# Linear-attention block and ReLU MLP on one core: four layer-norm tiles on GpSimd and a new order of all engines

## The chip, the cores and the metric

The kernel runs on one core of a Trainium2 chip. A core has a tensor engine (PE) with its weight loads (PEld), a vector engine (DVE), a scalar engine (ACT), GpSimd (POOL) and a sync engine (SP), which here issues all DMAs. The metric is the device time of one launch in microseconds (us). Before the change the median of three runs is 174.51 us (174.1 to 175.42).

## The reference

The input x has 2048 rows of 512 bf16 numbers. The block is a linear attention with 32 heads of 16 columns on the layer norm of x, and then a ReLU MLP with 1792 hidden columns on the layer norm of the sum h; both layer norms have no weights.

```python
def _layernorm(x, axis=-1, eps=1e-5):
    ...
    return (x - m) / jnp.sqrt(v + eps)
...
phi = lambda t: jnp.where(t > 0, t + 1, jnp.exp(t)) + 1e-6
pq, pk = phi(q), phi(k)
kv = jnp.einsum("bhsd,bhse->bhde", pk, v)
z = jnp.einsum("bhsd->bhd", pk)
num = jnp.einsum("bhqd,bhde->bhqe", pq, kv)
den = jnp.einsum("bhqd,bhd->bhq", pq, z)[..., None] + 1e-6
...
h = x + _A_ref(_layernorm(x, axis=-1), A_wqkv, A_wo)
h2 = h + _B_ref(_layernorm(h, axis=-1), B_w1, B_w2)   # relu(LN(h) @ w1) @ w2
```

## The kernel before

The 2048 rows are 16 tiles of 128 rows, and four chunks of four tiles. Nothing loops: the text ORDER lists some 560 words, and the last lines of the kernel call one function per word (`S.4` calls `op_S(4)`, L215). Each engine runs its own words in the order in which they stand; between engines only data, buffers and PSUM banks make one wait for the other. The last number of a PE word is its PSUM bank, of which there are eight.

First layer norm, tile t: `lx` loads x; `S` and `A` (DVE) take mean and variance; `R` (ACT, a logarithm and an exponential, here called the deviation) gives 1/deviation for one or two tiles; `N` (DVE, L229) writes (x minus mean) times 1/deviation into ln_nat, which is the tile h_nat in the profile. The normalised tile is then transposed into lnT: tiles 0 to 5 by PE (`T`) with a copy out of PSUM by ACT (`E`) or DVE (`V`), tiles 6 to 15 by a DMA that SP issues (`X`, L269).

Keys: `K` (PE, four 128x512 matmuls) gives x wk of a tile; `F` (ACT exponential), `U` (ACT ReLU), `M` (DVE minimum) and `D` (DVE sum) make phi of it; `G` (PE, four matmuls) gathers the product of the normalised tile and phi(k) in banks 4 to 7 over all tiles. Queries: `Q`, `qF`, `qU`, `qM`, `qD` do the same by chunk and quarter of the columns. `z` sums phi(k) over rows, `kv`, `kx`, `m` and `mD` fold wv, the head mask and wo into the matrix m_sb. `masks` (POOL) builds the three masks that `kx`, `zr`, `zh` and `rp` read.

The denominators: for chunk 0 by `d4`, `dl4`, `dx4` and `rp`; for the others `d` (PE), `dl` (ACT logarithm), `dx` (ACT exponential), `dm` (DVE product). `h` (PE) multiplies with m_sb, `hD` (DVE) adds x. Second layer norm: `s`, `a`, `r`, and `n` takes the mean off; `t` with `e` or `v`, or the DMA `x`, transpose. The MLP: `p` (PE, four matmuls for one of 14 blocks of 128 hidden columns of a chunk), evacuated in pairs by ACT (`pA`) or DVE (`pD`) with ReLU; `f` (PE) multiplies with w2; `fo` (DVE) scales by 1/deviation and adds h; `fd` stores a tile. Weight loads are `lk`, `lq`, `lv`, `lo`, `l1`, `l2`; `warm` are matmuls on zeros at the start.

SP issues the DMAs in one row in the order of the words. Each of its DMAs also takes one of eight completion counters in turn.

Of the kernel before, what the change touches and what calls it, by code (L numbers as in the profile page):

```python
# [18 lines left out]
table const masks warm.9.7 lx.0.1 S.0 lx.1.1 S.1 A.0 A.1 lx.2.2 S.3 S.2 R.1.1 R.0.1 lx.4.2 lk.0.2 lk.2.2  # L19
lx.6.2 A.3 A.2 N.0.2.2 N.0.0.2 N.1 R.2.2 N.2 N.3 warm.1.7 T.0.3.2.2 T.0.0.0.2 T.1.1 T.2.2 E.0.2.2 E.1 V.0.0.2  # L20
T.3.3 E.2 E.3 K.0.0 S.4 S.5 A.4 A.5 K.1.1 K.3.3 K.2.2 F.0.1 R.4.2 U.0.1 F.1.1 S.6 S.7 M.0.1 A.7 A.6 N.4 R.6.2
U.1.1 lx.8.4 T.4.0 D.0.1 G.0 M.1.1 N.5 N.7 T.5.1 E.4 U.2.1 F.2.1 E.5 F.3.1 U.3.1 K.4.0 D.1.1 S.9 N.6 S.8 G.1
M.2.1 A.9 A.8 D.2.1 R.8.2 K.5.1 F.4.2 U.4.2 M.3.1 S.10 N.8 D.3.1 N.9 M.4.2 S.11 D.4.2 lq.2.2 lq.0.2 lx.12.4
A.11 A.10 X.7 X.6 X.9 X.8 lv.0.2 G.2 K.7.3 K.6.2 G.3 F.6.2 R.10.2 U.6.2 S.12 S.13 M.6.2 N.11 N.10 A.13 A.12
D.6.2 R.12.2 G.4 G.5 K.9.1 K.8.0 F.8.2 U.8.2 S.14 N.13 A.14 N.12 S.15 M.8.2 A.15 D.8.2 X.11 X.10 R.14.2 N.14
N.15 lv.2.2 X.12 X.13 X.14 X.15 l1.0.2 l2.0.7 l2.7.7 lo.2.2 lo.0.2 l1.2.2 G.6 G.7 K.11.3 K.10.2 F.10.2 U.10.2
G.8 G.9 K.12.0 K.13.1 F.12.2 U.12.2 M.10.2 D.10.2 G.10 K.14.2 K.15.3 F.14.2 M.12.2 M.14.2 D.12.2 Q.0.1.1
Q.0.0.0 G.11 G.12 qF.0.0.2 qU.0.0.2 U.14.2 G.13 Q.0.3.1 Q.0.2.0 qM.0.0.2 D.14.2 qD.0.0.2 G.14 G.15 z.1.2
qF.0.2.2 qU.0.2.2 gD.0.2 z.0.2 z.2.2 z.3.2 zc qM.0.2.2 gA.2.2 zr zh qD.0.2.2 Q.1.1.3 Q.1.0.2 qF.1.0.2 qU.1.0.2
kv.1.4 kv.0.4 kv.2.4 kv.3.4 kx qM.1.0.2 Q.1.3.1 m.1.5 m.0.4 d4.0.3 m.3.7 m.2.6 Q.1.2.0 Q.2.0.2 dl4.0 mD.0.2  # L30
# [490 lines left out]
```

## Time and profile before

| | us |
|---|---|
| median of three runs (range) | 174.51 (174.1 to 175.42) |
| profiled execution, span from first to last instruction | 173.1 |
| PE busy | 165.8 |
| weight loads busy | 77.7 |
| DVE busy | 99.7 |
| ACT busy | 72.3 |
| POOL busy | 4.7 |

Of the profiled execution only its span is recorded; the runs' median lies 1.4 us above it. Busy time is the sum of the instructions' spans. A matmul's span (379 ns for 128x512) overlaps the next one's, so the spacing of matmuls, not their mean, tells how long a group takes: four 128x512 matmuls follow each other within 0.863 us once PE is at speed (2.16 us for ten in the chain of work that ended last), and the warm-up matmuls within 0.43 us each. The granted TensorE clock is 1.00 in every stage. An instruction on DVE or ACT likewise starts up to 0.1 us before the one ahead of it has ended. In the views, L12 is line 12 of the kernel, an arrow names what ended an engine's idle time, and SPq is SP's queue of DMA issues.

### The profile page before, as it was taken

What the parts mean: (1) busy time and instruction counts of PE and PEld (TensorE: products, weight loads), DVE (VectorE), ACT (ScalarE), POOL (GpSimd) and SP (SyncE); (2) the same over time, 40 slices, a digit from 0 to 9 for tenths busy, and PEclk for the clock granted to TensorE, in tenths of its full rate; (3) what the DMA queues carried; (4) which work ended last, traced back from release to release, by engine and by line L of the source; (5) the groups of instructions that cost most, each with busy time, mean ns of one, the idle gap of its engine ahead of it and who ended that gap; (6) DMA issues with size and microseconds to landing.
All of it is one profiled execution on the core that took longest, in us unless ns stands there. A gap on an engine that the chain in (4) does not pass through costs nothing.

```text
span 173.1 us, 2263 instructions
## 1 busy us (share of the span) xinstructions
PE 165.8 (96%) x856; PEld 77.7 (45%) x872; DVE 99.7 (58%) x208; ACT 72.3 (42%) x112; POOL 4.7 (3%) x21
## 2 busy tenths in 40 slices
PE   7699989999999999999999999999999999999992
PEld 2244434446444544444444444444444444444551
DVE  3899965154799949796338089455769402500032
ACT  2499755666586794213057210006623000363100
POOL 7300000000000000000000000000000000000000
PEclk9999999999999999999999999999999999999999
DMA  5883456899000000002220000462001320010021
GB/s 139 280 307 61 77 132 152 255 364 360 4 0 0 4 0 0 0 0 61 61 64 30 0 2 0 108 78 91 0 0 30 65 60 0 30 62 0 0 80 45
DMA packets 19979, 13.00 MB, mean 75 GB/s; under 512 B 12544, under 2 KB 18816, under 8 KB 19968
## 3 DMA queue, kind: packets, MB, share of 16 engines
q1 hardware_dynamic: 19968, 12.85, 26.5%
q8 instruction: 7, 0.11, 0.3%
q14 instruction: 4, 0.03, 0.1%
HBM read 7.86 MB, written 2.10 MB: 58 GB/s over the span
## 4 chain that ended last, share of the span: by engine, by line
PE 85%; DVE 7%; DMA 5%; issue 1%; SPq 1%
PE bk L470 28%; PE bk L450 28%; PE bk L435 8%; PE bk L285 8%; PE bk L329 5%; PE bk L277 4%; DVE st L215 4%; DMA lnT<-h_nat 2%; DMA x_nat<-in_A_x_dram 2%; DVE h_nat L229 2%; PE bk L415 2%; PE bk L337 1%; DVE eb L302 1%; PE bk L374 1%; PE bk L248 1%
## 5 line engine op out<-in xcount | busy, mean ns | idle before, releaser
L450 PE MATMUL bk<-lnT,w_sb 128*128 128x512 bf16 x220 | 50.9, 379 | 0.2
L470 PE MATMUL bk<-w_sb,at 128*128 128x512 bf16 (+1 forms) x233 | 49.8, 366 | 0.3
L470 PEld LDWEIGHTS <-at 128*128 128x128 bf16 x238 | 23.3, 98 | 25.3
L450 PEld LDWEIGHTS <-w_sb 128*128 128x128 bf16 x224 | 21.9, 98 | 26.5
L456 ACT ACTIVATE at<-bk 128x1024 bf16<-128x1024 f32 x14 | 14.2, 1022 | 41.0 <-PE bk L450 22.3
L478 DVE SCALAR_TENSOR_TENSOR gT<-bk,rstd,h_nat 128x512 bf16<-128x512 f32 (+1 forms) x17 | 11.8, 716 | 30.4 <-PE bk L470 17.0
L461 DVE TENSOR_SCALAR at<-bk 128x1024 bf16<-128x1024 f32 x14 | 17.1, 1221 | 14.4 <-PE bk L450 14.4
L295 ACT ACTIVATE eb<-bk 128x1024 bf16<-128x1024 f32 (+1 forms) x18 | 16.6, 930 | 10.4 <-PE bk L277 6.1
L418 ACT ACTIVATE ld<-bk,eps 128x512 f32<-128x512 f32 x12 | 7.7, 693 | 27.7 <-PE bk L415 27.7
L298 ACT ACTIVATE rb<-bk 128x1024 bf16<-128x1024 f32 (+1 forms) x18 | 16.6, 927 | 1.3 <-DVE pqs L408 0.7
L277 PE MATMUL bk<-wk_sb,lnT 128*128 128x512 bf16 x64 | 15.3, 379 | 0.6 <-DMA lnT<-h_nat 0.6
L441 DVE TENSOR_TENSOR h_nat<-bk,x_nat 128x512 bf16<-128x512 f32 x16 | 10.7, 682 | 8.6 <-PE bk L435 8.6
L435 PE MATMUL bk<-m_sb,pqs 128*128 128x512 bf16 x62 | 15.2, 379 | 0.1
L285 PE MATMUL bk<-lnT,wq_sb 128*128 128x512 bf16 x61 | 14.7, 379 | 0.1
L329 PE MATMUL bk<-at,h_nat 128*128 128x512 bf16 x55 | 13.2, 379 | 0.1
L215 DVE BATCH_NORM_STATS2 st<-x_nat 128x6 f32<-128x512 bf16 x16 | 10.5, 680 | 2.7 <-DMA x_nat<-in_A_x_dram 2.7
L302 DVE TENSOR_SCALAR eb<-eb 128x1024 bf16<-128x1024 bf16 (+1 forms) x18 | 6.9, 389 | 7.0 <-ACT eb L295 7.0
L217 DVE BATCH_NORM_STATS2 st<-h_nat 128x6 f32<-128x512 bf16 x16 | 10.7, 683 | 0.2
L435 PEld LDWEIGHTS <-pqs 128*128 128x128 bf16 x64 | 6.3, 98 | 7.5
L277 PEld LDWEIGHTS <-lnT 128*128 128x128 bf16 x64 | 6.1, 98 | 7.9 <-DMA lnT<-h_nat 1.0
L329 PEld LDWEIGHTS <-h_nat 128*128 128x128 bf16 x64 | 6.2, 98 | 7.3
L285 PEld LDWEIGHTS <-wq_sb 128*128 128x128 bf16 x64 | 6.0, 98 | 6.9 <-issue 0.2
(63 smaller groups left out, 95.2 us busy)
## 6 DMA issues: line engine op xcount, KB each, us to landing
w_sb<-in_B_w_dram SPq DMA_DIRECT2D x4, 896.0 KB, 8.1
out_dram<-gT SPq DMA_DIRECT2D x15, 128.0 KB, 1.8
x_nat<-in_A_x_dram SPq DMA_DIRECT2D x2, 512.0 KB, 7.0
x_nat<-in_A_x_dram SPq DMA_DIRECT2D x3, 256.0 KB, 4.0
wk_sb<-in_A_wqkv_dram SPq DMA_DIRECT2D x2, 256.0 KB, 4.8
wq_sb<-in_A_wqkv_dram SPq DMA_DIRECT2D x2, 256.0 KB, 6.8
wv_sb<-in_A_wqkv_dram SPq DMA_DIRECT2D x2, 256.0 KB, 3.3
wo_sb<-in_A_wo_dram SPq DMA_DIRECT2D x2, 256.0 KB, 8.9
```

Of the source, the lines that this page charges most:

```text
L215: op_S = lambda t: nc.vector.bn_stats(out=st[:, t, :], in_=x_nat[:, t, :])
L277: nc.tensor.matmul(bk[:, b, :], lhsT=lnT[c][:, kd, j * P : (j + 1) * P], rhs=wk_sb[:, kd, :], start=(kd == 0), stop=(kd == KD - 1),)
L285: nc.tensor.matmul(bk[:, b, :], lhsT=wq_sb[:, kd, j * P : (j + 1) * P], rhs=lnT[c][:, kd, :], start=(kd == 0), stop=(kd == KD - 1),)
L295: nc.scalar.activation(out=buf(eb, kind, i, n), in_=bank(at_bank[kind, i], n), func=ACT.Exp)
L298: nc.scalar.activation(out=buf(rb, kind, i, n), in_=bank(at_bank[kind, i], n), func=ACT.Relu)
L329: nc.tensor.matmul(bk[:, KD + kd, :], lhsT=ln_nat[:, t, kd * P : (kd + 1) * P], rhs=pk(t)[:, 0, :], start=(t == 0), stop=(t == NT - 1),)
L435: nc.tensor.matmul(bk[:, b, :], lhsT=pqs[:, (c * KD + jb) % NQ, j * P : (j + 1) * P], rhs=m_sb[:, jb, :], start=(jb == 0), stop=(jb == KD ...
L450: nc.tensor.matmul(bk[:, b, :], lhsT=w1_sb[:, kd, f * P : (f + 1) * P], rhs=lnT[c][:, kd, :], start=(kd == 0), stop=(kd == KD - 1),)
L456: nc.scalar.activation(out=acts[c % 2][:, f : f + n, :], in_=bank(at_bank["p", c, f], n), func=ACT.Relu)
L461: nc.vector.tensor_scalar(out=acts[c % 2][:, f : f + n, :], in0=bank(at_bank["p", c, f], n), scalar1=0.0, scalar2=None, op0=ALU.max,)
L470: nc.tensor.matmul(bk[:, b, 0 : w * P], lhsT=acts[c % 2][:, f, j * P : (j + 1) * P], rhs=w2_sb[:, f, k * P : (k + w) * P], start=(f == 0), ...
L478: nc.vector.scalar_tensor_tensor(out=o_t[:, t % NO, cols], in0=bk[:, at_bank["f", t, k], 0 : w * P], scalar=rstd2[:, t : t + 1], in1=h_nat ...
```

## The change

Two functions are new in use: `ng` writes minus the mean of a tile on GpSimd, and `Np` normalises a tile on GpSimd as (x plus minus mean) times 1/deviation, in one instruction of 128x512 bf16 with two per-row scalars. Tiles 4, 6, 7 and 8 take this way; the other twelve stay on DVE. `ng` stands in the order for twelve tiles, of which eight (5, 9 to 15) have no `Np`, so that their result is read by nothing. `masks` moves from the start of GpSimd's row to behind the `ng` of tile 14.

All the other words are put in a new order, with other banks in places. In the row of PE the kinds and numbers of instructions stay. Tiles 2 and 5 are now copied out of PSUM by DVE (`V`) instead of ACT, and tile 0 in both halves by ACT. Of the 28 evacuations of the MLP's hidden blocks ACT does 19 and DVE 9, where each did 14. SP loads the last four tiles of x ahead of wq; wq's two halves, wv's two and one of wo's now stand between the DMA transposes, where before only wv's two did. `dx4` writes to the place of wk, which is no longer used then, instead of rd.

The diff also adds functions and options that the new order doesn't call (a sum for `z` on DVE, a broadcast of denominators through DRAM, `p` in column halves, `dm` over several blocks); they are left out here.

```diff
 ORDER = """
-table const masks warm.9.7 lx.0.1 S.0 lx.1.1 S.1 A.0 A.1 lx.2.2 S.3 S.2 R.1.1 R.0.1 lx.4.2 lk.0.2 lk.2.2
-lx.6.2 A.3 A.2 N.0.2.2 N.0.0.2 N.1 R.2.2 N.2 N.3 warm.1.7 T.0.3.2.2 T.0.0.0.2 T.1.1 T.2.2 E.0.2.2 E.1 V.0.0.2
-T.3.3 E.2 E.3 K.0.0 S.4 S.5 A.4 A.5 K.1.1 K.3.3 K.2.2 F.0.1 R.4.2 U.0.1 F.1.1 S.6 S.7 M.0.1 A.7 A.6 N.4 R.6.2
-U.1.1 lx.8.4 T.4.0 D.0.1 G.0 M.1.1 N.5 N.7 T.5.1 E.4 U.2.1 F.2.1 E.5 F.3.1 U.3.1 K.4.0 D.1.1 S.9 N.6 S.8 G.1
-M.2.1 A.9 A.8 D.2.1 R.8.2 K.5.1 F.4.2 U.4.2 M.3.1 S.10 N.8 D.3.1 N.9 M.4.2 S.11 D.4.2 lq.2.2 lq.0.2 lx.12.4
-A.11 A.10 X.7 X.6 X.9 X.8 lv.0.2 G.2 K.7.3 K.6.2 G.3 F.6.2 R.10.2 U.6.2 S.12 S.13 M.6.2 N.11 N.10 A.13 A.12
-D.6.2 R.12.2 G.4 G.5 K.9.1 K.8.0 F.8.2 U.8.2 S.14 N.13 A.14 N.12 S.15 M.8.2 A.15 D.8.2 X.11 X.10 R.14.2 N.14
-N.15 lv.2.2 X.12 X.13 X.14 X.15 l1.0.2 l2.0.7 l2.7.7 lo.2.2 lo.0.2 l1.2.2 G.6 G.7 K.11.3 K.10.2 F.10.2 U.10.2
-G.8 G.9 K.12.0 K.13.1 F.12.2 U.12.2 M.10.2 D.10.2 G.10 K.14.2 K.15.3 F.14.2 M.12.2 M.14.2 D.12.2 Q.0.1.1
-Q.0.0.0 G.11 G.12 qF.0.0.2 qU.0.0.2 U.14.2 G.13 Q.0.3.1 Q.0.2.0 qM.0.0.2 D.14.2 qD.0.0.2 G.14 G.15 z.1.2
-qF.0.2.2 qU.0.2.2 gD.0.2 z.0.2 z.2.2 z.3.2 zc qM.0.2.2 gA.2.2 zr zh qD.0.2.2 Q.1.1.3 Q.1.0.2 qF.1.0.2 qU.1.0.2
-kv.1.4 kv.0.4 kv.2.4 kv.3.4 kx qM.1.0.2 Q.1.3.1 m.1.5 m.0.4 d4.0.3 m.3.7 m.2.6 Q.1.2.0 Q.2.0.2 dl4.0 mD.0.2
-dx4.0 qU.1.2.2 qF.1.2.2 mD.2.2 rp.0.1.5 rp.0.2.6 rp.0.3.7 rp.0.0.4 Q.2.1.3 Q.2.3.1 Q.2.2.0 qU.2.0.2 qU.2.2.2
-qF.2.0.2 qF.2.2.2 qD.1.0.2 rm.0.0.2 qM.1.2.2 rm.0.2.2 qD.1.2.2 h.1.5 h.0.4 hD.1 s.1 hD.0 h.3.7 Q.3.0.2 h.2.6
-...
-p.3.1.1 p.3.0.0 pA.3.0.2 f.10.6.7.7 pD.3.2.2 p.3.4.0 p.3.5.1 p.3.6.2 p.3.7.3 fo.9 pA.3.4.2 p.3.9.1 fo.10 fo.11
-pA.3.6.2 fd.9 fd.11 fd.10 p.3.8.0 f.12.4.0.7 pA.3.8.2 p.3.12.0 p.3.10.2 p.3.13.1 pA.3.12.2 r.12.4 p.3.11.3
-pA.3.10.2 f.13.5.0.7 f.13.5.7.7 f.12.4.7.7 fo.12 fd.12 fo.13 fd.13 f.15.7.0.14.0.2 f.14.6.0.7 f.14.6.7.7
-fo.15.0.2 fo.14 fd.15.0.2 fd.14 f.15.4.0.14.2.2 fo.15.2.2 fd.15.2.2
+lx.1.1 const lx.0.1 S.1 table A.1 S.0 A.0 R.1.1 R.0.1 N.1 lx.2.2 warm.9.7 T.1.5 S.3 N.0.0.2 S.2 A.3 A.2 lk.0.2
+lx.4.2 T.0.0.0.2 warm.1.7 N.0.2.2 E.1 lk.2.2 T.0.3.2.2 S.4 R.2.2 E.0.0.2 E.0.2.2 K.1.2 N.3 lx.6.2 S.5 A.4 A.5
+lx.8.4 N.2 T.3.1 E.3 ng.4.1 R.4.2 S.7 K.0.7 Np.4 T.2.5 K.3.3 F.0.1 N.5 T.5.1 U.0.1 U.1.1 A.7 V.2 T.4.4 K.2.7
+S.6 V.5 A.6 E.4 R.6.2 F.2.1 F.1.1 U.2.1 S.8 M.0.1 S.9 lx.12.4 D.0.1 M.1.1 D.1.1 A.9 M.2.1 A.8 ng.7.1 ng.6.1
+Np.6 Np.7 K.4.0 K.5.1 X.6 U.3.1 F.3.1 G.0 D.2.1 X.7 R.8.2 G.1 G.2 S.10 M.3.1 A.10 S.11 A.11 D.3.1 N.9 U.4.2
+F.4.2 R.10.2 S.12 ng.8.1 K.6.2 K.7.3 N.11 M.4.2 D.4.2 S.15 N.10 S.13 G.3 U.6.2 Np.8 X.8 lq.2.2 K.8.0 G.4 A.15
+A.12 A.13 F.6.2 R.12.2 M.6.2 N.13 N.12 X.9 G.5 K.9.1 F.8.2 lq.0.2 X.11 D.6.2 S.14 A.14 R.14.2 U.8.2 X.10
+lv.2.2 X.12 K.11.3 G.6 N.15 K.10.2 N.14 M.8.2 D.8.2 G.7 X.13 lv.0.2 X.14 lo.2.2 X.15 l2.7.7 U.10.2 F.10.2
+K.12.0 K.13.1 G.8 K.14.2 G.9 K.15.3 U.12.2 F.12.2 l2.0.7 l1.0.2 lo.0.2 l1.2.2 M.10.2 D.10.2 F.14.2 M.12.2
+D.12.2 M.14.2 Q.0.1.1 G.10 ng.13.1 G.11 U.14.2 D.14.2 z.3.2 z.1.2 z.0.2 z.2.2 G.12 Q.0.0.0 qF.0.0.2 qU.0.0.2
+G.13 G.14 G.15 gA.2.2 zc gD.0.2 qM.0.0.2 qD.0.0.2 Q.0.2.0 Q.0.3.1 qF.0.2.2 kv.3.4 kv.2.4 ng.10.1 ng.5.1
+ng.14.1 masks kv.1.4 kv.0.4 ng.15.1 qU.0.2.2 Q.1.1.3 Q.1.0.2 kx qM.0.2.2 zh qD.0.2.2 zr ng.11.1 ng.9.1 ng.12.1
+m.3.7 m.2.6 d4.0.1 m.1.5 m.0.4 qF.1.0.2 Q.1.2.0 dl4.0 qU.1.0.2 mD.2.2 Q.1.3.1 Q.2.1.3 mD.0.2 dx4.0 rp.0.2.6
+rp.0.3.7 rp.0.0.4 qM.1.0.2 Q.2.0.2 rp.0.1.5 qU.1.2.2 qF.1.2.2 qD.1.0.2 rm.0.2.2 rm.0.0.2 qM.1.2.2 qF.2.0.2
+qU.2.0.2 Q.2.3.1 Q.2.2.0 h.2.7 h.0.2 qU.2.2.2 qF.2.2.2 h.3.5 h.1.4 d.1.1.6 qD.1.2.2 hD.2 s.2 hD.0 Q.3.1.3
+Q.3.0.2 dl.1.1 a.2 hD.3 s.0 hD.1 s.3 a.0 n.2 Q.3.3.1 dx.1.1 Q.3.2.0 t.2.5 qU.3.0.2 a.3 s.1 a.1 n.1 n.0 n.3
+t.1.7 qF.3.0.2 t.0.3 e.2 t.3.2 e.0 qF.3.2.2 qU.3.2.2 v.1 d.1.0.4 d.1.2.6 d.1.3.7 v.3 dl.1.3 dl.1.2 qM.2.0.2
+qD.2.0.2 p.0.1.3 p.0.0.2 dm.1.1 qM.2.2.2 pD.0.0.2 qM.3.0.2 d.2.1.5 dx.1.3 dl.2.1 dx.1.2 dl.1.0 dx.2.1 dx.1.0
+p.0.2.0 p.0.3.1 p.0.4.2 p.0.5.3 pD.0.2.2 dm.1.2 qD.2.2.2 qM.3.2.2 p.0.6.0 p.0.7.1 pA.0.4.2 dm.1.3 dm.1.0
+d.2.0.2 dl.2.0 h.4.3 d.2.2.5 d.2.3.6 h.7.7 pD.0.6.2 dx.2.0 h.6.2 dl.2.3 dl.2.2 hD.4 qD.3.2.2 qD.3.0.2 dm.2.1
+hD.6 p.0.9.3 d.3.0.6 h.5.1 d.3.1.5 p.0.8.2 s.4 hD.5 p.0.11.1 d.3.3.4 p.0.10.0 dx.2.3 pD.0.8.2 dl.3.1 dx.3.1
+dx.2.2 dl.3.3 p.0.13.3 dl.3.0 d.3.2.5 p.0.12.2 r.0.4 dm.2.2 hD.7 dm.2.3 dm.2.0 s.6 a.4 n.4 s.5 s.7 a.7 n.7 a.6
+pA.0.10.2 dx.3.0 pA.0.12.2 f.0.4.0.7 n.6 f.0.4.7.7 h.10.6 x.4 x.7 dm.3.0 x.6 h.8.3 dl.3.2 dx.3.2 dx.3.3 hD.8
+hD.10 dm.3.2 a.5 dm.3.1 dm.3.3 h.9.1 f.1.5.0.7 n.5 x.5 h.11.3 s.10 fo.0 s.8 hD.9 a.10 hD.11 r.4.4 f.1.5.7.7
+h.13.4 h.15.6 p.1.0.0 p.1.3.3 p.1.1.1 a.8 fo.1 h.12.5 f.3.7.0.7 hD.15 pD.1.0.2 s.9 h.14.6 p.1.4.0 p.1.5.1
+p.1.2.2 f.3.7.7.7 a.9 n.8 hD.13 pD.1.2.2 pA.1.4.2 hD.14 p.1.6.2 p.1.7.3 p.1.12.0 p.1.13.1 s.14 hD.12 s.15 s.13
+a.14 fo.3 a.15 n.10 s.11 a.13 a.11 pA.1.6.2 f.4.4.0.7 f.2.6.0.7 r.8.4 pA.1.12.2 n.14 n.9 n.15 n.11 n.13 s.12
+a.12 f.2.6.7.7 n.12 fo.2 p.1.8.0 p.1.9.1 f.6.6.0.7 p.1.11.3 p.1.10.2 f.5.5.0.7 pA.1.8.2 pD.1.10.2 x.11 x.10
+x.9 x.12 x.8 x.15 p.2.5.1 p.2.4.0 f.4.4.7.7 f.5.5.7.7 pA.2.4.2 p.2.12.0 p.2.13.1 fd.3 fd.0 fd.1 fd.2 x.13
+p.2.3.3 f.7.7.0.7 pA.2.12.2 p.2.1.1 p.2.2.2 pA.2.2.2 x.14 p.2.0.0 f.7.7.7.7 p.2.6.2 f.6.6.7.7 p.2.7.3 pA.2.6.2
+fo.7 fo.4 pD.2.0.2 fo.5 p.3.9.1 p.3.8.0 p.2.11.3 p.2.10.2 f.9.5.0.7 pA.3.8.2 pA.2.10.2 p.2.9.1 p.2.8.0
+f.8.4.0.7 p.3.7.3 pD.2.8.2 fo.6 f.10.6.0.7 p.3.6.2 f.9.5.7.7 p.3.4.0 p.3.5.1 pA.3.6.2 pA.3.4.2 p.3.2.2
+f.10.6.7.7 p.3.12.0 f.8.4.7.7 p.3.3.3 p.3.13.1 f.11.7.0.7 pA.3.2.2 fd.6 fd.7 fd.5 pA.3.12.2 fo.9 p.3.0.0
+p.3.1.1 fd.9 fd.4 f.11.7.7.7 fo.10 fo.8 fo.11 p.3.10.2 p.3.11.3 fd.11 fd.8 fd.10 pA.3.0.2 pA.3.10.2 r.12.4
+f.13.5.0.7 f.15.7.0.14.0.2 f.12.4.0.7 f.12.4.7.7 f.14.6.0.7 f.14.6.7.7 f.13.5.7.7 fo.15.0.2 fo.12 fo.13 fo.14
+fd.15.0.2 fd.12 fd.13 fd.14 f.15.4.0.14.2.2 fo.15.2.2 fd.15.2.2
 """
@@ -128,6 +130,7 @@
     st = big.tile([P, NT, nc.vector.BN_STATS_DIM], F32, name="st")
     mv = big.tile([P, NT, nc.vector.BN_AGGR_DIM], F32, name="mv")
     rstd = big.tile([P, NT], F32, name="rstd")
+    nmean = big.tile([P, NT], F32, name="nmean")
     st2 = big.tile([P, NT, nc.vector.BN_STATS_DIM], F32, name="st2")
     mv2 = big.tile([P, NT, nc.vector.BN_AGGR_DIM], F32, name="mv2")
     rstd2 = big.tile([P, NT], F32, name="rstd2")
 o_t = gT
+r4 = wk_sb
...
@@ -221,6 +227,17 @@
         nc.scalar.activation(out=dst, in_=var, func=ACT.Ln, bias=eps5[:], scale=1.0)
         nc.scalar.activation(out=dst, in_=dst, func=ACT.Exp, scale=-0.5)
 
+    def op_ng(t, n):
+        nc.gpsimd.tensor_scalar(
+            out=nmean[:, t : t + n], in0=mv[:, t : t + n, 0], scalar1=-1.0, scalar2=None, op0=ALU.mult
+        )
+
+    def op_Np(t):
+        nc.gpsimd.tensor_scalar(
+            out=ln_nat[:, t, :], in0=x_nat[:, t, :],
+            scalar1=nmean[:, t : t + 1], scalar2=rstd[:, t : t + 1], op0=ALU.add, op1=ALU.mult,
+        )
+
     op_R = lambda t, n: rstd_of(rstd[:, t : t + n], mv[:, t : t + n, 1])
     op_r = lambda t, n: rstd_of(rstd2[:, t : t + n], mv2[:, t : t + n, 1])
 
 def op_dx4(c):
-    nc.scalar.activation(out=rd[:, c % 2, :], in_=ld[:, c % 2, :], func=ACT.Exp, scale=-1.0)
+    nc.scalar.activation(out=r4[:, c, :], in_=ld[:, c % 2, :], func=ACT.Exp, scale=-1.0)
...
 def op_rp(c, jb, b):
...
-        bk[:, b, :], lhsT=erep[rows, :], rhs=rd[rows, c % 2, :], start=True, stop=True
+        bk[:, b, :], lhsT=erep[rows, :], rhs=r4[rows, c, :], start=True, stop=True
```

## Prediction

> **What bounds the kernel now.** I read the page first, then the waits of the tensor engine, then stage windows, then SP's queue. The page and the waits:
>
> ```profile
> PE 165.8 (96%) x856; PEld 77.7 (45%) x872; DVE 99.7 (58%) x208; ACT 72.3 (42%) x112; POOL 4.7 (3%) x21
> ```
>
> ```profile
> PE bk L248 <- DVE h_nat L229: 1.6, 1, 1.6
> PE bk L212 <- DVE ones L174: 1.2, 1, 1.2
> PE bk L277 <- DMA lnT<-h_nat: 0.6, 1, 0.6
> ```
>
> PE is the bound. After its warm-up matmuls it waits twice: 1.6 us for the first normalised tile (first transpose at 7.25 us) and 0.6 us at 22.8 us for the DMA transpose of tile 8. From there to 170.1 us it never waits again. The new order keeps every PE instruction (same count of each kind), so it can only move these two waits, the DVE and DMA tail behind the last matmul, or add waits. Two windows show where engines off PE have no slack:
>
> ```profile
> 8.70:17.00 8.30, 8.25 (x48) 4.06 (x47) 8.30 (x27) 7.98 (x20) 0.00 (x0) 1.00 0.58 190
> 17.00:23.00 6.00, 5.45 (x26) 2.30 (x25) 5.99 (x18) 4.03 (x8) 0.00 (x0) 1.00 0.46 102
> ```
>
> The columns are length, then busy us of PE, weight loads, DVE, ACT, POOL. Up to 23 us DVE is busy throughout (8.30 of 8.30, 5.99 of 6.00) and ACT nearly so; POOL is empty. Work taken off DVE there is worth something, if what takes its place isn't later.
>
> **The change, part by part.**
>
> *Normalisation on POOL.* Tiles 4, 6, 7, 8 leave DVE. Rows for both sides:
>
> ```profile
> L229 DVE TENSOR_SCALAR h_nat<-x_nat,mv,rstd 128x512 bf16<-128x512 bf16 x15 | 5.6, 401 | 0.0
> L229 DVE TENSOR_SCALAR h_nat<-x_nat,mv,rstd 128x256 bf16<-128x256 bf16 x2 | 0.6, 329 | 0.0
> L178 POOL TENSOR_SCALAR_AFFINE_SELECT mask<-mask 128x128 bf16<-128x128 bf16 x2 | 0.7, 342 | 0.1
> L184 POOL MEMSET mask<- 128x128 bf16 x1 | 0.2, 206 | 0.0
> L505 POOL MEMSET const-float32-0.0<- 128x1 f32 x1 | 0.1, 99 | 0.3 <-issue 0.3
> ```
>
> Back to back a DVE normalisation takes about 0.33 us (timeline: a pair in 0.73), so DVE gets back 4 x 0.33 = 1.3 us, and pays 0.56 us net for one more PSUM copy that ACT gives up (two of 0.42 against one of 0.28). POOL's 128x512 pass is in no trace. Memsets of 1 and 128 elements give (206-99)/127 = 0.84 ns per element, so 0.53 us for 512; the mask select, which reads as well as writes, gives (342-99)/127 = 1.9, so 1.08 us. I take 1.0, near the select, since both read. The negations are 128x1, 0.1 us each; eight of the twelve feed nothing. The masks' 4.9 us of POOL (1.31 to 6.20 us) move behind tile 14's statistics, at about 23 us; they would be done by 29 and are first used at about 44: free.
>
> *Front.* I walk the new order with measured spacings (statistics 0.61, aggregate 0.1 to 0.17, DVE normalisation 0.33, a 128x512 ACT pass 0.48, 1/deviation 0.5, four matmuls 0.863). S.1, A.1, S.0, A.0 run before the wait for tiles 2 and 3, so N.1 ends at 5.0 us, where before it stood behind that wait. But S.3 waits for its load (5.46) with N.0 queued behind it, and T.0's second half comes at 7.45. The first key matmul goes at 7.6, not 8.71, but has two transposes fewer behind it (0.44) and waits for the second half of wk (sixth on SP as before, landing 8.45): 0.4. T.3 8.88, K.0 9.1, T.2 9.97, K.3 10.19, T.5 11.05. Tile 4's deviation stands on ACT behind E.3 (ends 9.75), so it is there at 10.2; POOL writes tile 4 by 11.25, and T.4 is due at 11.27: hidden, barely. Then K.2, K.4, K.5, G.0, G.1, G.2 without a wait, ending at 16.67. Before, the same work ended at 16.93. **Gain 0.26 us.**
>
> *SP's queue.* Ten tiles are transposed by DMA. The relevant rows, SP's timeline and the issues:
>
> ```profile
> 17.35 1.19 SPq L269 DMA_TRANSPOSE lnT<-h_nat  x1
> 18.59 1.26 SPq L269 DMA_TRANSPOSE lnT<-h_nat  x1
> 19.90 0.58 SPq L201 DMA_DIRECT2D wv_sb<-in_A_wqkv_dram  x1
> ```
>
> ```profile
> lnT<-h_nat SPq DMA_TRANSPOSE x10, 2.5
> ```
>
> A transpose keeps SP for 1.31 us with its gap and lands 2.5 us after its issue; a weight load between two of them costs 0.65. Before, the chain began at 13.06, had two loads inside, and issued tile 15 at 28.6 (landed 31.0, used at 32.34). The new order moves wq's two loads, and the first half of wo, between the transposes: five loads inside. Tile 6's deviation needs E.4 and A.6 and ends at 12.7; POOL ends tile 6 at 13.75, tile 7 at 14.75, and tile 8 (deviation at 15.55) at 16.65. So X.6 at 13.8, X.7 15.1, X.8 16.7, load, X.9 18.65, load, X.11 20.6, X.10 21.9, load, X.12 23.85, X.13 25.15, load, X.14 27.1, load, X.15 29.05, landing 31.5. PE reaches tile 15 at 30.5 by its own work from 16.67 on (nine K and seven G before it, 0.863 each); it would start at about 31.5. Before, it stood at 32.34 with one G more done (0.86): 31.47. **The lead is gone.** Behind each of two loads of before a transpose was late (tile 8 landed after 4.2 us, tile 11 kept SP for 1.71); with five I add 0.3.
>
> *Middle.* The new order leaves shorter covers. Q.2.3 needs a bank that ACT frees after the exponentials of chunk 1: about 0.2 us late. d.2.0 needs bank 2, freed by an ACT evacuation standing behind four logarithm and exponential pairs (1.09 each) and two 128x1024 passes: 0.15. The transpose of tile 8 in the second half is fifth in SP's row and lands some 0.4 us ahead of its use: nothing. Five evacuations move from DVE (1.22) to ACT (1.02), both under 65% busy behind 61 us: nothing. Before has no wait here, so nothing can be gained.
>
> *Tail.* Before (timeline), DVE writes tile 14 while the last 14 half-width matmuls run, waits 0.78, and only one half tile stands behind the last matmul:
>
> ```profile
> 168.56 0.75 DVE L478 SCALAR_TENSOR_TENSOR gT<-bk,rstd,h_nat 128x512 bf16<-128x512 f32 x1 [2.54 <-PE bk L470]
> 170.09 0.48 DVE L478 SCALAR_TENSOR_TENSOR gT<-bk,rstd,h_nat 128x256 bf16<-128x256 f32 x1 [0.78 <-PE bk L470]
> ```
>
> Now f.13 ends next to last and DVE has tiles 13 and 14 to write (0.72 each) while those 14 run (1.53): 0.1 late, and the last store issues 0.45 us behind tile 14's. I add 0.15.
>
> **Sum:** -0.26 + 0.26 + 0.3 + 0.35 + 0.15 = +0.8 us on the profiled span of 173.1, so 173.9; the median of the three runs lies 1.4 above the span: 175.3.
>
> **Rivals.**
>
> *POOL and DVE get in each other's way (slower).* The rows show DVE's normalisation costing (401-329)/256 = 0.28 ns per element against 1.33 for its statistics, so it reads several elements at a time; before, POOL's work ends at 6.2 us and DVE's first such pass is at 6.88, so no row shows both at once. If one waits for the other whole: tile 4's POOL pass waits 0.35 for N.5; tiles 6 and 7 hold D.0 and M.1 for 0.4 and 1.0, D.1 comes at 15.5 instead of 14.03 and G.1 waits 0.65; A.8 and with it tile 8's deviation come 1.2 later, and so X.8 and every transpose behind it. Tile 15 is then at 32.8: 1.3 us on the forecast, **176.6**, to 177.6 if masks and evacuations collide too. It decides from the point where a wait on DVE passes the 0.3 us of cover before G.0. The Trainium skill (SBUF — State Buffer, Who interferes with whom) says just this: VectorE and GpSimd share one port pair, locked for a whole instruction by a VectorE pass in a two-port mode, or against one with two SBUF inputs. By that rule the time is this rival's; no run here shows it yet.
>
> *The lead holds (faster).* POOL's pass costs 0.53, X.6 starts 0.45 sooner, transposes behind loads land in 2.5, and tile 15 starts at 30.9: -0.55, nothing lost later, tail 0.1: **174.0**. Even with all of the 0.6 us wait and the 1.1 us of earlier start kept, PE's fixed work leaves about 172.8.
>
> **Chances.** Forecast 0.48, of it 0.04 over 1%; collisions 0.37, of it 0.33 over 1%; lead kept 0.15, of it 0.06 beyond 1%. One per cent (1.75 us) is about what the runs, 174.1 to 175.42, can tell from nothing. Faster 0.06, same 0.57, slower 0.37. The range goes from the lead kept (173.5) to collisions with the upper price (177.6).
>
> **What would show it.** Mean time of the 128x512 POOL pass (0.53 to 1.08); DVE's normalisation and minimum rows at 401 and 280 ns or longer beside POOL; PE waiting for lnT's DMA between 19 and 32 us by about 1 us in sum; X.15's issue at 29 us; no PE wait over 0.3 us behind 61 us. I am wrong if PE waits in the second half by more than that, if the first key matmuls run at the 0.43 us spacing of the warm-up ones, or if POOL's pass lies outside its bounds.

## The result and the profile after

The changed kernel takes 176.64 us (median of four runs, 176.52 to 177.97), the kernel before 174.31 on the same chip (173.97 to 175.42). The ratio is 1.0137 with a 95% interval of 1.0091 to 1.0183: slower by 1.4%. The profiled execution took 176.75, its span is 175.0, against 173.1 before.

First the page's line of busy times and the waits of the tensor engine (engine, line, what ended the wait, us in total, times, the longest), after:

```profile
PE 166.7 (95%) x856; PEld 77.1 (44%) x872; DVE 95.1 (54%) x200; ACT 76.9 (44%) x116; POOL 11.9 (7%) x37
```

```profile
PE bk L294 <- DMA lnT<-h_nat: 2.0, 3, 1.6
PE bk L218 <- DVE ones L180: 1.2, 1, 1.2
PE bk L265 <- DVE h_nat L246: 0.9, 2, 0.5
```

PE is still the bound, with the same 856 instructions. The wait for the first normalised tile has shrunk from 1.6 us to 0.9 in two pieces, as the new order meant. The wait for DMA transposes has grown from 0.6 to 2.0 in three pieces. The timeline of PE shows where they are (start, length, then the instruction; in brackets the idle time before it and what ended it):

```profile
21.90 1.04 PE L294 MATMUL bk<-wk_sb,lnT 128*128 128x512 bf16 x4 [0.16 <-DMA lnT<-h_nat]
24.49 1.04 PE L294 MATMUL bk<-wk_sb,lnT 128*128 128x512 bf16 x3 [1.55 <-DMA lnT<-h_nat]
...
32.88 1.04 PE L294 MATMUL bk<-wk_sb,lnT 128*128 128x512 bf16 x4 [0.28 <-DMA lnT<-h_nat]
```

These are the keys of tiles 9, 11 and 15. The stage windows of after (length; busy us of PE, weight loads, DVE, ACT, POOL; granted clock, DMA share, GB/s):

```profile
8.70:17.00 8.30, 8.25 (x47) 3.77 (x47) 8.22 (x23) 7.92 (x18) 4.47 (x8) 1.00 0.37 115
17.00:23.00 6.00, 5.67 (x25) 2.10 (x24) 5.66 (x17) 3.03 (x8) 0.63 (x3) 1.00 0.71 154
23.00:33.20 10.20, 8.38 (x37) 3.57 (x39) 5.41 (x11) 6.29 (x8) 6.13 (x20) 1.00 0.69 153
```

The last stretch in the kernel before:

```profile
23.00:33.20 10.20, 10.15 (x47) 4.61 (x47) 4.29 (x10) 6.20 (x8) 0.00 (x0) 1.00 0.62 150
```

From 23 to 33.2 us PE is now busy for 8.38 of 10.20 us; before, it was busy for 10.15 of them. That is where the time was lost. The cause is in SP's timeline, whose rows are DMA issues:

```profile
16.20 1.19 SPq L286 DMA_TRANSPOSE lnT<-h_nat  x1
17.44 0.58 SPq L207 DMA_DIRECT2D wq_sb<-in_A_wqkv_dram  x1
18.11 1.91 SPq L286 DMA_TRANSPOSE lnT<-h_nat  x1
20.07 0.57 SPq L207 DMA_DIRECT2D wq_sb<-in_A_wqkv_dram  x1
20.73 3.13 SPq L286 DMA_TRANSPOSE lnT<-h_nat  x2
...
29.06 0.60 SPq L207 DMA_DIRECT2D wo_sb<-in_A_wo_dram  x1
29.70 1.19 SPq L286 DMA_TRANSPOSE lnT<-h_nat  x1
```

Transposes with nothing in front take 1.19 to 1.30 us of SP and land 2.4 to 2.5 us after their issue (tiles 6, 7 and 8). The one behind the first half of wq, tile 9, takes 1.91 and lands after 3.75; the one behind the second half, tile 11, takes 1.82 and lands after 3.71, at 24.44, where PE has stood since 22.9. Tiles 12, 14 and 15, each behind a load, take the usual 1.2 but land after 3.09, 2.82 and 3.12. Tile 15 is issued at 29.70 and is there at 32.83; before it was there at 31.05.

The long rows of tiles 9 and 11 aren't the price of a load alone. The DMA activity of after from 18 to 24 us also has two entries of instruction queues (queue, packets, MB, share of the window):

```profile
q14 instruction: 1, 0.01, 1.2%
q8 instruction: 1, 0.02, 1.1%
```

The first runs from 18.67 to 19.84, within the issue of tile 9, the second from 21.02 to 22.11, within that of tile 11. Experiments 1 and 12 show what such an entry does without a load in front.

The new work on GpSimd, in the groups of instructions by shape (out and in, shapes, number | busy us, mean ns of one | idle time before):

```profile
L246 DVE TENSOR_SCALAR h_nat<-x_nat,mv,rstd 128x512 bf16<-128x512 bf16 x11 | 4.3, 407 | 0.9 <-ACT rstd L228 0.9
...
L236 POOL TENSOR_SCALAR h_nat<-x_nat,nmean,rstd 128x512 bf16<-128x512 bf16 x4 | 3.5, 866 | 1.4 <-POOL nmean L231 1.4
...
L231 POOL TENSOR_SCALAR nmean<-mv 128x1 f32<-128x1 f32 x12 | 2.6, 232 | 16.6 <-DVE mv L222 16.5
...
L319 DVE TENSOR_SCALAR eb<-eb 128x512 bf16<-128x512 bf16 x4 | 1.5, 370 | 0.0
```

A pass costs POOL 0.87 us, a negation 0.23. The minimum on DVE (the last row) took 280 ns before; more of that below.

**Where the 1.9 us of span came from.** I set the start of equal PE work side by side. At the start of the keys of tiles 6 and 7, with the same keys and G groups done in both, the new kernel is 0.83 us ahead (16.10 against 16.93). At the keys of tile 15 it is 1.4 behind (32.88 against 31.47, the start of before less the one G that it had done more). From there to 62 us it loses another 0.4, and behind the last matmul 0.05. The sum is 1.9.

### The profile page after: what moved, and what is told of

The parts are those of the page before. It is cut to its first block, busy times and chain, and to the rows that moved or that the text cites. A ratio compares the mean times of both kernels' runs of the same rounds, so it can differ in the third digit from the quotient of the medians.

```text
span 175.0 us, 2277 instructions
## 1 busy us (share of the span) xinstructions
PE 166.7 (95%) x856; PEld 77.1 (44%) x872; DVE 95.1 (54%) x200; ACT 76.9 (44%) x116; POOL 11.9 (7%) x37
## 4 chain that ended last, share of the span: by engine, by line
PE 79%; DVE 10%; DMA 4%; SPq 3%; issue 2%; ACT 1%
PE bk L493 28%; PE bk L513 28%; PE bk L302 8%; PE bk L477 8%; DVE st L221 4%; PE bk L346 3%; DVE h_nat L246 2%; DMA x_nat<-in_A_x_dram 2%; DMA lnT<-h_nat 2%; PE bk L455 2%; SPq L286 1%; DVE at L322 1%; PE bk L365 1%; DVE eb L319 1%; DVE mv L222 1%
## 5 line engine op out<-in xcount | busy, mean ns | idle before, releaser
L493 PE MATMUL bk<-lnT,w_sb 128*128 128x512 bf16 x219 | 51.8, 379 | 0.3
L513 PE MATMUL bk<-w_sb,at 128*128 128x512 bf16 (+1 forms) x233 | 51.6, 367 | 0.3
L499 ACT ACTIVATE at<-bk 128x1024 bf16<-128x1024 f32 x19 | 19.3, 1020 | 54.7 <-PE bk L493 54.7
L504 DVE TENSOR_SCALAR at<-bk 128x1024 bf16<-128x1024 f32 x9 | 11.0, 1223 | 17.3 <-PE bk L493 17.3
L319 DVE TENSOR_SCALAR eb<-eb 128x1024 bf16<-128x1024 bf16 (+1 forms) x18 | 7.4, 411 | 5.8 <-ACT eb L312 5.8
L294 PEld LDWEIGHTS <-lnT 128*128 128x128 bf16 x64 | 5.5, 98 | 9.9 <-DMA lnT<-h_nat 4.6
```

The source lines that it names most:

```text
L294: nc.tensor.matmul(bk[:, b, :], lhsT=lnT[c][:, kd, j * P : (j + 1) * P], rhs=wk_sb[:, kd, :], start=(kd == 0), stop=(kd == KD - 1),)
L493: nc.tensor.matmul(bk[:, b, cols], lhsT=w1_sb[:, kd, f * P : (f + 1) * P], rhs=lnT[c][:, kd, cols], start=(kd == 0), stop=(kd == KD - 1),)
L499: nc.scalar.activation(out=acts[c % 2][:, f : f + n, :], in_=bank(at_bank["p", c, f], n), func=ACT.Relu)
L504: nc.vector.tensor_scalar(out=acts[c % 2][:, f : f + n, :], in0=bank(at_bank["p", c, f], n), scalar1=0.0, scalar2=None, op0=ALU.max,)
L513: nc.tensor.matmul(bk[:, b, 0 : w * P], lhsT=acts[c % 2][:, f, j * P : (j + 1) * P], rhs=w2_sb[:, f, k * P : (k + w) * P], start=(f == 0), ...
```

## The experiments

Each ratio is that of the kernel's time to the kernel before, run on the same chip in turn, with its 95% interval. Of each edit the diff shows SP's row or the words of ORDER that it touches.

**1. The loads out of the transposes.** The new kernel, but wq is loaded ahead of all transposes, wv and the first half of wo behind them.

```diff
-lx.12.4 X.6 X.7 X.8 lq.2.2 X.9 lq.0.2 X.11 X.10 lv.2.2 X.12 X.13 lv.0.2 X.14 lo.2.2 X.15
+lx.12.4 lq.2.2 lq.0.2 X.6 X.7 X.8 X.9 X.11 X.10 X.12 X.13 X.14 X.15 lv.2.2 lv.0.2 lo.2.2
```

> The changed kernel with the five weight loads taken out from between the DMA transposes: wq's two halves go right behind the last load of x, wv's two and wo's first half behind the transpose of tile 15. GpSimd's four normalisations and the order of all other engines stay. Theory L (loads between transposes make the transposes behind them slow to issue and to land, 1.8 to 1.9 us and 3.1 to 3.75 us instead of 1.2 and 2.45): the transposes issue 1.3 us apart, tensor engine no longer waits for lnT's DMA (2.0 us in the changed kernel), time 174.0 to 174.8. Rival P (GpSimd and VectorE hinder each other, and this reaches the tensor engine): the time stays at 176.0 or above.

Measured 1.0001 (0.9965 to 1.0037): the whole loss is gone. Tile 15 is now issued at 26.96. One wait for a transpose is left, in the waits of PE:

```profile
PE bk L294 <- DMA lnT<-h_nat: 0.9, 1, 0.9
```

It is that of tile 11, issued at 19.13, which landed only after 4.3 us although no load is near it. The next one, tile 10, keeps SP for 2.04 us, also without a load. The landing of tile 11, and the row of tile 10:

```profile
DMA to landing us min/median/max: 4.3/4.3/4.3
```

```profile
20.74 2.04 SPq L286 DMA_TRANSPOSE lnT<-h_nat  x1
```

So without the loads there is no loss, and something else makes one transpose late and another slow to issue.

**2. The normalisation on GpSimd alone.** The order of before, with tiles 4, 6, 7 and 8 on GpSimd in the places where DVE had them.

```diff
-... N.4 ... N.6 ... N.7 ... N.8
+... ng.4.1 Np.4 ... ng.6.1 Np.6 ... ng.7.1 Np.7 ... ng.8.1 Np.8
```

> The old order, with one part of the change alone: tiles 4, 6, 7 and 8 are normalised on GpSimd, each with its negated mean right ahead of it, in the places where VectorE normalised them. Masks stay at the start, loads where they were. Theory L: GpSimd's pass of 0.9 us is 0.5 us longer than VectorE's; tile 4's transpose on the tensor engine comes 0.3 to 0.5 us later, the DMA transposes of tiles 7 and 6 0.3 us later, which 1.7 us of idle time ahead of tile 9's transpose covers: 174.3 to 175.0. Rival P: 175.5 or above, the sum of VectorE passes held up beside GpSimd's.

Measured 0.9909 (0.9872 to 0.9946): faster. The part of the change that I feared, GpSimd beside DVE, is the part that gains.

**3. The new order without GpSimd.** DVE normalises all tiles, at the same words; the negations go.

```diff
-ng.4.1 ... Np.4 ... Np.6 ... Np.7 ... Np.8
+N.4 ... N.6 ... N.7 ... N.8
```

> The changed kernel without GpSimd's normalisations: VectorE normalises tiles 4, 6, 7 and 8 at the same places of the order, the negated means are gone, all else stays. Theory L: the five loads still stand between the transposes, so the time stays at 176.2 to 177.0; VectorE takes 1.3 us more at 9 to 17 us. Rival P: with the hindrance gone the time falls to 174.8 to 175.5.

Measured 1.0386 (1.031 to 1.0462), more than any theory expected. DVE reaches tile 8 late, its transpose is issued at 22.96 instead of 16.20, that of tile 15 at 35.99, and PE waits 4.6 us for transposes. The new order needs GpSimd. Part of the loss is the clock: behind a wait of 3.4 us for tile 8 the profile has PE at half of it (0.50 in the row, after the engines' busy times) for 6.7 us:

```profile
24.30:31.00 6.70, 5.56 (x14) 1.93 (x15) 1.58 (x4) 0.00 (x0) 0.00 (x0) 0.50 0.73 155
```

At full clock those 5.56 us of work would have taken about half, an estimate from this row. How much of the loss is DVE's longer row, and how much the place of tile 8 in it (behind work that waits), this run doesn't separate.

**4. The loads between the transposes of the old order.** The kernel before, with five loads between the transposes.

```diff
-lq.2.2 lq.0.2 lx.12.4 X.7 X.6 X.9 X.8 lv.0.2 X.11 X.10 lv.2.2 X.12 X.13 X.14 X.15 l1.0.2 lo.2.2
+lx.12.4 X.7 X.6 lq.2.2 X.9 lq.0.2 X.8 X.11 X.10 lv.0.2 X.12 X.13 lv.2.2 X.14 lo.2.2 X.15 l1.0.2
```

> The kernel before, with one part of the change alone: wq's two halves, wv's two and wo's first half are put between the DMA transposes at the places that they have in the changed kernel (behind the second, third, fifth, seventh and eighth transpose). Nothing else changes, GpSimd does no normalisation. Theory L: the transpose of tile 8 lands at about 23.6 us instead of 22.8 and that of tile 15 at about 33 instead of 31.05, the tensor engine waits 1.0 to 1.7 us more for them: 175.2 to 176.0. Rival P: no change, 174.3.

Measured 1.0114 (1.007 to 1.0158): the old order loses nearly as much by the loads as the new kernel does. The waits of PE, and the landing of tile 8 behind the second half of wq (with the entries of both instruction queues in flight too, q8 from 22.82 and q14 from 22.91, so the 5.6 isn't the load's alone):

```profile
PE bk L276 <- DMA lnT<-h_nat: 2.4, 1, 2.4
```

```profile
DMA to landing us min/median/max: 5.6/5.6/5.6
```

Together with the first experiment this shows the loads as the cause in both orders.

**5. Tile 8 ahead of tile 9.** Tile 8 is the late transpose of the old order. On top of experiment 2 it goes first, and wv's loads go behind all transposes.

```diff
-X.9 X.8 lv.0.2 X.11 X.10 lv.2.2 X.12 ... X.15 | K.9.1 K.8.0
+X.8 X.9 X.11 X.10 X.12 ... X.15 lv.0.2 lv.2.2 | K.8.0 K.9.1
```

> The old order with GpSimd's four normalisations (the second experiment's kernel) and three further moves in it: the transpose by DMA of tile 8 ahead of that of tile 9, tile 8's key matmuls ahead of tile 9's, and wv's two loads behind the transpose of tile 15, so that no load is left between the transposes. Theory L: the remaining wait of 0.3 to 0.9 us on the transpose of tile 8 goes, 0.985 to 0.990 of the kernel before. Rival (the transposes are late at about 20 to 24 us whatever stands beside them, since a transpose was late there in the first experiment too): 0.990 to 0.993, as in the second experiment.

A miss: 1.0006 (0.997 to 1.0043), and the gain of experiment 2 is lost. Tile 8 is no longer late; tile 9, which now stands at that time (19.43), lands after 4.70 us and holds PE for 1.0. The lateness belongs to a time, not to a tile or a load.

**6. The new front, the old rest.** Experiment 1's order up to the keys, with the masks at the start and the eight unread negations left out; from the queries on, the words of before.

```diff
-(from the queries on) the words of after
+(from the queries on) the words of before; masks at the start; no ng for tiles 5 and 9 to 15
```

> The new order of the changed kernel up to the last G (loads out from between the transposes as in the first experiment, masks at the start, the eight unused negated means gone), and the old order for all words from the queries on. Against the first experiment's kernel (1.000 of the kernel before) it has the old middle, second half and tail. If the new order behind 33 us costs what the first experiment didn't give back: 0.990 to 0.994. If the new front itself is worth no more than the old front with GpSimd: 0.997 to 1.001.

Measured 1.0006 (0.997 to 1.0043). In the profiles PE ends 0.4 us earlier than in experiment 1 (169.81 against 170.23): this is the price of the new middle as one profile of each shows it. The times of the two kernels are too scattered to confirm a difference of 0.4. The wait for tile 11 is there again: issued 19.16, landed after 4.25.

**7. Three more warm-up matmuls in the kernel before.** They fill PE's idle time ahead of the first transpose.

```diff
-warm.9.7
+warm.12.7
```

> The kernel before with twelve warm-up matmuls on zeros ahead of the first transpose instead of nine, and nothing else; they fill the tensor engine's idle time from 5.7 to 7.2 us. Theory C (in some executions the first key matmuls run at half speed, since the clock comes up later; these are the ones listed with a granted clock of 0.99): fewer such executions, median 0.992 to 0.997. Rival: the three matmuls only fill idle time, 1.000.

Measured 0.9974 (0.995 to 0.9999). The median, 174.40, is that of the launches of before at full clock (174.39). What goes is the slow first keys, told below; five launches of before of 175.4 to 175.7 at full clock have no counterpart here either, and why isn't known.

**8. The masks at the start.** The new kernel with the masks where they were and without the unread negations.

```diff
-... ng.14.1 ... masks
+masks ... (no ng for tiles 5 and 9 to 15)
```

> The changed kernel with the masks back at the start of GpSimd's row and without the eight negated means that nothing reads; all else stays. Theory L (both were hidden): 1.011 to 1.016, as the changed kernel. Rival P (late masks hold VectorE up beside them at 24 to 31 us): 1.005 or less.

Measured 1.0129 (1.0083 to 1.0174), as the new kernel itself. Neither the masks' new place nor the eight negations cost anything that shows.

**9. GpSimd alone, with more warm-up.** Experiments 2 and 7 together.

```diff
-warm.9.7 ... N.4 ... N.6 ... N.7 ... N.8
+warm.12.7 ... ng.4.1 Np.4 ... ng.6.1 Np.6 ... ng.7.1 Np.7 ... ng.8.1 Np.8
```

> The second experiment's kernel (old order, tiles 4, 6, 7 and 8 on GpSimd) with the twelve warm-up matmuls of the seventh, so that launches with a slow first stage no longer hide what GpSimd is worth. The seventh experiment alone was 0.9974 of the kernel before. If GpSimd's normalisations are worth about 1 us by themselves: 0.987 to 0.992. If what the second experiment showed was the clock's luck: 0.996 to 0.999.

Measured 0.9903 (0.9869 to 0.9937), 174.0 us: faster than experiment 7, and against the kernel before not to be told from experiment 2 (0.9909). Its span is 172.2. Tile 8 still comes late (issued 17.45, landed after 4.4), and PE waits 0.3 for it.

**10. A G group ahead of the late tile.** In experiment 9, G.6 (0.86 us of PE) goes before the keys of tile 8, to cover the wait.

```diff
-K.9.1 K.8.0 G.6
+K.9.1 G.6 K.8.0
```

> The kernel of e9_pool_warm with G of tile 6 put ahead of the key matmuls of tile 8 on the tensor engine, so that 0.86 us of work that is ready lies where the tensor engine waited for the transpose of tile 8 (issued at 18 to 19 us and landed 4.2 to 4.7 us later in every kernel so far). If that late transpose is what holds the old order: 0.5 to 0.9 us less than e9_pool_warm. If the next transposes are late in the same way and take its place: no change against it.

A miss: 0.9901 (0.9873 to 0.9929), no different from experiment 9. The wait for the transpose is gone and one of 0.2 us for a phi(k) of DVE has come; with 0.3 to win and 0.2 given back, nothing is left that can be measured.

**11. Only wq's two loads out.** The new kernel; wv and wo stay between the transposes.

```diff
-lx.12.4 X.6 X.7 X.8 lq.2.2 X.9 lq.0.2 X.11 X.10 lv.2.2
+lx.12.4 lq.2.2 lq.0.2 X.6 X.7 X.8 X.9 X.11 X.10 lv.2.2
```

> The changed kernel with only wq's two loads moved behind the last load of x; wv's two and wo's first half stay between the transposes. Theory L: wq's two loads delay the transposes of tiles 9 and 11 (waits of 0.2 and 1.6 us in the changed kernel), the other three those of tiles 12 to 15 (wait of about 0.3 us): most comes back, 1.001 to 1.005 of the kernel before. If each of the five costs alike: 1.008.

Measured 1.0042 (1.001 to 1.0074): slower than with all five out (1.0001), less slow than with all five in (1.0137, on another chip). So both groups of loads seem to have a part. Which is the larger isn't settled: the twelve times lie between 175.68 and 177.69, and in the profile a wait of 0.8 us for wk's load, which the other profiles don't have, stands beside one of 0.8 for the transposes.

**12. The instruction fetch moved.** The traces of before, after and experiments 1, 2, 4 to 7 and 9 each have an entry of queue q8, 16 KB of instructions, between 19.3 and 22.8 us, when PE has done 170 to 184 matmuls and weight loads; the late transposes of before and of experiments 1, 4, 5, 6 and 9, and tiles 9 and 11 of after, were in flight then. To move it, 34 one-column matmuls on zeros take the place of four warm-up matmuls in experiment 9: 60 more PE instructions with their weight loads, in time that was idle, and nothing else.

```diff
-warm.12.7
+warm.8.7 tick.34.7
...
+    op_tick = n matmuls of zeros[:, 0:P] by zeros[:, 0:1] into bank 7
```

> The kernel of e9_pool_warm with eight of its twelve warm-up matmuls and 34 matmuls of one column on zeros added behind them: 60 more instructions on the tensor engine ahead of its first transpose. In every kernel so far a DMA of 16 KB on the instruction queue runs when the tensor engine has done 170 to 184 matmuls and weight loads, at 19.3 to 22.8 us, and the transpose issued 1.4 to 3 us before it lands after 3.8 to 5.6 us. Theory I (this fetch of instructions holds the transpose up): the fetch comes 6 to 7 us sooner, at 13 to 15 us; the transpose of tile 7 or 6 now lands after 3.5 us or more, and that of tile 8 after 2.4 to 2.8. Rival W (wv's first load right behind it, or the place in the order, makes the transpose of tile 8 late): it lands after 4.0 us or more again.

The DMA activity of experiment 9 from 19 to 21 us, and of this run from 14 to 15.4 (queue, packets, MB, share of the window):

```profile
q8 instruction: 1, 0.02, 4.4%
```

```profile
q8 instruction: 1, 0.02, 5.1%
...
lnT<-h_nat SPq DMA_TRANSPOSE x2, 3.4
```

The fetch came at 14.19 instead of 19.33, and the lateness moved with it. Tile 7, issued at 13.22, now lands after 3.7 us, and tile 8 after 2.4 where it took 4.4. Tile 6, issued at 14.63 with no load in front, takes 1.76 us of SP. The landing of tile 8 in experiment 9, then here:

```profile
DMA to landing us min/median/max: 4.4/4.4/4.4
```

```profile
DMA to landing us min/median/max: 2.4/2.4/2.4
```

PE's waits for transposes are gone. So the fetch, not the load behind the transpose or DVE's work, makes that one late. In time (one run, 174.23 us, on another chip) nothing was won over experiment 9, whose wait was 0.3; here PE waited 0.6 for wk.

## Why the prediction was right and where it failed

The forecast was 175.3 us with a range of 173.5 to 177.6; 176.64 lies in the range and 1.3 above the forecast. "Within 1%" had the largest chance, and it is slower by 1.4%. The number is that of the rival (176.6), but the mechanism is the forecast's, with one term too small.

*SP's queue: the step that failed.* The prediction walked SP's row for five loads and had tile 15 issued at 29.05 and there at 31.5, with 0.3 more for transposes behind loads: 31.8 in all. The row was half a microsecond ahead of the walk at tile 9 (18.11 against 18.65) and 0.75 behind it two transposes later, at tile 10 (22.65 against 21.9); tile 15 was issued at 29.70 and there at 32.83. The term named "with five I add 0.3" was the mis-sized one: it measured 1.3, half in the time of issue (tiles 9 and 11 took 1.9 and 1.8 us of SP instead of 1.2), half in the landing of tile 15 (3.1 us instead of 2.5).

The two halves have different causes, and the prediction had only one of them. Over the fourteen profiles, 77 transposes have neither a load in front nor an instruction entry in flight: they take 1.19 to 1.31 us of SP and land after 2.4 to 2.6. The 19 issued within 0.2 us of a load, with no such entry in flight, take 1.2 and land after 2.8 to 3.1. So a load costs its 0.65 in the row, which the walk had, and 0.2 to 0.7 in the landing behind it. The 15 of 140 that keep SP for more than 1.35 us were all issued beside an entry of q8 or q14, with a load in front or without one. The prediction read the row of tile 11 before as the price of a load, but the fetch of q8 from 20.54 to 21.58 lay in it:

```profile
20.95 1.71 SPq L269 DMA_TRANSPOSE lnT<-h_nat  x1
```

It also put tile 8's 4.2 us down to a load, though the load stood behind that tile; experiments 9 and 12 show that this one is the instruction fetch. The term that the sum lacked is the fetch. Whether a load makes a fetch last longer isn't separated: the entry of q14 took 1.17 us in after, beside wq's load, and 0.31 in experiment 1.

That the loads between the transposes make the loss is shown by experiments 1 and 4. Without them the fetch is still there, but tile 15 is issued 2.7 us sooner (26.96 against 29.70), and that room covers it.

*Front.* Predicted 0.26 us ahead at 16.67; measured 0.83. The second half of wk, walked at 8.45, was there at 7.06, so the wait of 0.4 for it didn't come (with the same front in experiment 11 it came at 8.63, and PE waited 0.8), and the transposes behind the first keys went at 8.09 and not at 8.88. This changed nothing in the end: behind 22.9 us PE stands where SP's row puts it, and a larger lead was a longer wait. In experiment 1, without the loads, the lead is given back at tile 11, which the fetch makes late (0.9 of wait).

*GpSimd's pass.* Taken as 1.0 us, with bounds of 0.53 and 1.08; measured 0.77 to 1.05, mean 0.87. The negations cost 0.23 and not 0.1. The masks ended at 30.6, were first used later, and were free (experiment 8). The saving on DVE was costed at 1.3 us and credited to the path only through the front. Experiment 2 shows that it is worth more by itself than I gave it, up to 0.9%.

*The rival: GpSimd and DVE get in each other's way.* What it says of the hardware is in the rows. DVE's timeline of after, and POOL's:

```profile
13.21 0.28 DVE L319 TENSOR_SCALAR eb<-eb 128x512 bf16<-128x512 bf16 x1
13.53 0.80 DVE L322 TENSOR_TENSOR pk_lo<-rb,eb 128x512 bf16<-128x512 bf16 x1
...
15.64 0.68 DVE L319 TENSOR_SCALAR eb<-eb 128x512 bf16<-128x512 bf16 x1
```

```profile
12.25 1.80 POOL L236 TENSOR_SCALAR h_nat<-x_nat,nmean,rstd 128x512 bf16<-128x512 bf16 x2 [0.45 <-POOL nmean L231]
...
15.40 0.77 POOL L236 TENSOR_SCALAR h_nat<-x_nat,nmean,rstd 128x512 bf16<-128x512 bf16 x1 [0.22 <-POOL nmean L231]
```

The DVE product at 13.53 takes 0.80 us and the minimum at 15.64 takes 0.68, and each ends 0.15 to 0.3 us after POOL's pass beside it (14.05 and 16.17). Experiment 3 has the same words without GpSimd, and its groups have the two at their old price:

```profile
L318 DVE TENSOR_SCALAR eb<-eb 128x512 bf16<-128x512 bf16 x4 | 1.1, 277 | 0.0
...
L321 DVE TENSOR_TENSOR pk_lo<-rb,eb 128x512 bf16<-128x512 bf16 x2 | 0.8, 417 | 0.0
```

The Trainium skill (SBUF — State Buffer, Who interferes with whom) says that VectorE and GpSimd share one port pair that one of them locks for a whole instruction; these rows agree, with 0.4 us for each of two collisions. GpSimd waits in turn: two of its four passes take 0.77 us, and the one during which the minimum of 13.21 runs takes 1.05. But the rival had them hold tile 8's deviation for 1.2 us and with it every transpose behind. Tile 8 was issued at 16.20, before the forecast's 16.7, so that didn't happen. Experiment 1 keeps the four passes and has no loss, and experiment 2, which has them in the old order, is faster. That the rival's number came out is chance.

*Middle and tail.* Middle predicted 0.35, measured 0.4 (and 0.4 between experiments 1 and 6). Behind 61 us there is no wait over 0.3, as said. The tail was predicted at 0.15 and is 0.05; DVE has three tiles to write in one go at the end:

```profile
170.39 2.01 DVE L521 SCALAR_TENSOR_TENSOR gT<-bk,rstd,h_nat 128x512 bf16<-128x512 f32 x3 [3.78 <-PE bk L513]
```

*The sum.* Predicted at tile 15 +0.3, middle 0.35, tail 0.15: 0.8. Measured 1.4, 0.4 and 0.05: 1.9.

**What stays open.** How much of experiment 3's loss is GpSimd's share, how much the place of tile 8 and how much the clock. Why experiment 5 gives back all of experiment 2's gain, when its wait for the transpose is only 0.7 us longer (1.0 against 0.3); by its launches at full clock it is even 0.8 us slower than the kernel before (175.15 against 174.39). What the new front's lead would be worth with the fetch moved and the loads out wasn't tried.

## What to carry to other kernels

Count what stands between the transposes in a DMA queue, and price a transpose behind a load by the rows that stand behind one, not by the median of all. Before a slow row is put down to its neighbour, look at every queue that ran beside it: here the slowest rows were those beside an instruction fetch, and a queue with no time to spare can't cover one. Five loads cost 1.4% in one order and 1.1% in another, and taking them out gave all of it back. Where a vector engine is full and GpSimd idle, a few of its passes may be moved even at more than twice their price (0.87 us against 0.33 to 0.40) and with collisions, if the passes that they hold have cover; change one thing at a time, since here the part that gained 0.9% was hidden in an order that lost more. When PE stands for a DMA, ask from where to where the next trace's lateness moves: if it stays at a time and not with a tile, look for other traffic on the DMA engines.

## What the runs showed of the hardware that I had not expected

*Instructions come through the DMA engines, and a transpose in flight pays for it.* A 16 KB fetch of PE's instructions delays one transpose from 2.4 us of landing to 3.7 to 4.7 where no load stands in front, and the one issued beside it can keep SP for up to 2.04 us instead of 1.2 (experiment 1). It comes by the count of PE instructions: 60 more of them at the start brought it 5.1 us earlier (experiment 12).

*The first keys run at half speed in some launches.* The same 16 matmuls of the first keys in the kernel before, then experiment 4's profile:

```profile
8.71 3.62 PE L277 MATMUL bk<-wk_sb,lnT 128*128 128x512 bf16 x16
```

```profile
8.69 4.67 PE L276 MATMUL bk<-wk_sb,lnT 128*128 128x512 bf16 x14
```

Fourteen of them here take more than sixteen there. In the second the granted clock had come up, fell back and came up again (1.00, 0.50, 1.00):

```profile
4.90:8.20 3.30, 1.54 (x14) 0.68 (x12) 2.93 (x10) 1.56 (x7) 1.11 (x4) 1.00 0.95 294
8.30:11.60 3.30, 3.30 (x13) 1.45 (x12) 3.04 (x10) 2.28 (x7) 0.00 (x0) 0.50 0.64 259
11.70:17.00 5.30, 5.25 (x31) 2.69 (x31) 4.80 (x16) 4.82 (x12) 0.00 (x0) 1.00 0.25 49
```

Launches like the second are listed with a granted clock of 0.99 and are 0.8 to 1.5 us longer in the median: in the kernel before 7 of 25 on one chip, 11 of 17 and 13 of 23 on two others. With three more warm-up matmuls in the idle time ahead there was none in 10 (experiment 7) and none in 6 (experiment 9). The Trainium skill (TensorE: Matmul & The Clock Gate, Part 1: The HAM clock gate) says that PE runs at half rate unless a free-running window of activity has been busy, so that the number of slow matmuls changes from run to run. The rows agree: the clock was at half for 3.4 us behind a wait of PE of 1.7 us. This bears on how the ratios are read: with full-clock launches alone (those listed at 0.997 or more) the gain of experiment 9 is 0.85 us (174.0 against 174.85, 0.5%) and that of experiment 2 is 1.1 (174.29 against 175.4, 0.6%); the rest of their 0.9% is the larger share of slow starts in the kernel before. Experiment 4, where 7 of 10 launches had slow first keys, loses 1.4 us by full-clock launches alone (176.8 against 175.4, 0.8%). The other way round, experiment 8 loses 2.9 us so (177.26 against 174.39, 1.6%) and experiment 11 1.6 us (176.47 against 174.85, 0.9%), more than their ratios say, since many launches of the kernel before beside them started slowly. Experiment 1 stays at nothing lost (175.36 against 175.4).

*GpSimd's selects pay too.* The second mask, built beside DVE's work in after, takes 551 ns for a 128x128 select where before, at the start, it took 310.
